# Denser filler work at the start, and another order of the mask, the gates and the router's product, in a fused mLSTM cell and mixture-of-depths kernel

## The chip, the cores and the metric

The kernel runs on one core of a Trainium2 chip. The metric is the device time of one execution in microseconds. Before the change it is 199.75 us, the median of three runs (199.61 to 199.81). The profile was taken of another execution, of 199.56 us; it spans 197.8 us from its first to its last instruction, and all positions in time below are counted from the start of that span.

A core has five engines that work side by side and wait for each other by semaphores. The profile calls them PE (TensorE, matrix products; PEld are its weight loads), DVE (VectorE), ACT (ScalarE), POOL (GpSimd) and SP (SyncE, which here issues transfers).

## The reference

Two blocks follow each other. The first is an mLSTM cell over 4 batches, 8 heads, 768 steps and a head dimension of 40:

```python
for t in range(S):
    m_new = np.maximum(f_gate[:, :, t] + m, i_gate[:, :, t])
    f_stab = np.exp(f_gate[:, :, t] + m - m_new)
    i_stab = np.exp(i_gate[:, :, t] - m_new)
    C = f_stab * C + i_stab * einsum('bhd,bhe->bhde', v_t, k_t)
    n = f_stab * n + i_stab * k_t
    y[:, :, t] = sigmoid(o_gate_t) * (C q_t) / max(|n . q_t|, 1)
```

The second is a mixture of depths on x, which is y with the heads side by side (4 x 768 x 320). Scores are x times a router's vector `w_gate`; in each batch the 128 rows of highest score go through a two-layer perceptron (320 to 1024 to 320, ReLU), and its output, times the sigmoid of the score, is added to them. All other rows are passed on.

## The kernel before

The kernel cuts each batch into 6 chunks of 128 steps, 24 chunks in all, and runs the recurrence in its chunked form. For a chunk it makes transposed q and k (`turn`, line 283, into T), their products pS (line 325), a matrix of decay weights W (`weights`, lines 303 and 304: a product pW of two small operands a_o and M_o, and an exponential on ScalarE), the causal mask of W (`causal`, line 309, GpSimd), the weighted products P (`weighted`, line 331, VectorE), the numerators pH (line 382), and the exchange with the state C (lines 351, 357, 364 to 374). The order of the program on each engine is the order in which the functions are called; each engine keeps it.

The prologue, which makes the first two chunks and the gates' running sums, is written out by hand, up to the first full `step`. Between its pieces stand fillers, products whose result nobody reads, which keep TensorE at work:

```python
def warm(n):
    pw = ps_c.tile([128, 4 * L], FP, name="pw", tag="c")
    for _ in range(n):
        nc.tensor.matmul(pw, earlier[:, 0:128], earlier[:, 0:4 * L], start=True, stop=True)
...
warm(6)
sums(0, nc.vector)                 # running sums of the gates, VectorE
maxima(0)
split(0, 1, nc.gpsimd)             # a in three bf16 parts
ends(0)                            # pe: three tiny products
warm(2)
split(0, 0, nc.vector, slice(0, BH))
carry(0)
T[0] = work.tile([128, 2, NP, L], FP, name="T")
turn(loaded[0][0], 0, T[0])        # four transposes of k, a copy by ScalarE
moving = operands(0, 0, [(ps_s, "s"), (ps_s, "s")], nc.vector)
moving()                           # M_o by VectorE
pm = carried(0)
turn(loaded[0][0], 1, T[0])        # the same of q
pg = ps_m.tile([128, DM], FP, name="pg", tag="m")
nc.tensor.matmul(pg, one, wg_row, start=True, stop=True)   # router's vector on all rows
...
W[0] = weights(0, 0)
causal(W[0])
level(0, pm)
split(0, 0, nc.vector)
pS[0] = products(T[0])
scales(0)                          # two exponentials, ScalarE
nc.scalar.copy(out=wg, in_=pg)
...
P[0] = weighted(pS[0], W[0])
...
moving = operands(0, 1, [(ps_m, "m"), (ps_m, "m")], nc.vector)
moving()
moving = operands(0, 2, [(ps_c, "c")], nc.vector)
...
turn(loaded[1][0], 0, T[1])
keep(0, columns(0))
```

`earlier` is a tile of ones, 128 x 768 in bf16, set by GpSimd; it is later the mask of the router's comparison, and the running sums read it too.

Operands of later chunks are made on ScalarE alone, as are the output gates:

```python
# operands(u, c, pools) without an engine: six small products into pO, then
nc.scalar.activation(out=a_o[u, c], in_=pO[1], func=AF.Identity, bias=of[:, 0:1], scale=1.0)
for h in range(4):
    nc.scalar.activation(out=M_o[u, c][:, h], in_=pO[0], func=AF.Identity, ...)

def gated(n):
    so = loaded[n][2]
    nc.scalar.activation(out=so, in_=so, func=AF.Tanh, scale=0.5)
    nc.scalar.add(so, so, 1.0)
```

In a step the outputs are scaled by the gates on GpSimd (`sor = so * rec`, line 397, in `norm`). The first full step is that of chunk 2, and is called with hooks:

```python
def step(n, first=False, **more):
    ...
    pH = within(P[n], v1)
    run(more.get("carry", ()))
    ...                                  # decay of C (POOL), products, exchange
    num, sor = norm(nums.get(n), pH, so)
    run(more.get("sor", ()))
    ...                                  # P and the state of the next chunk
    if n + 2 < N:
        stated(n + 2); W[n + 2] = weights(*steps[n + 2]); causal(W[n + 2])
    layer(b, c)                          # fillers, or the perceptron's products
    ... turned(n + 2) ... gated(n + 2) ... result, score, compare
    run(more.get("end", ()))
    if n == 2:
        operands(0, 5, [(ps_m, "m")])

def late():
    W[3] = weights(0, 3)
    operands(0, 4, [(ps_m, "m")])
    gated(2)
    gated(3)

step(2, first=True, carry=[late], sor=[lambda: causal(W[3])], end=[second_places])
```

So the mask of chunk 3 is called behind the scaling by the gates in this step.

Of the kernel before, what the change touches and what calls it, by code (L numbers as in the profile page):

```python
# [8 lines left out]
FP = mybir.dt.float32  # L9
BF = mybir.dt.bfloat16  # L10
# [11 lines left out]
def kernel(  # L22
# [20 lines left out]
    nc = tc.nc  # L43

    B, H, S, D = q.shape
    L = 128
# [4 lines left out]
    DM = H * D  # L51
# [15 lines left out]
    const = ctx.enter_context(tc.tile_pool(name="const", bufs=1))  # L67
# [8 lines left out]
    ps_h = ctx.enter_context(tc.tile_pool(name="ps_h", bufs=1, space=PSUM))  # L76
    ps_m = ctx.enter_context(tc.tile_pool(name="ps_m", bufs=2, space=PSUM))
# [6 lines left out]
    def load_gates(eng, dst, src, g):  # L84
        for c in range(3):
            t = slice((3 * g + c) * L, (3 * g + c + 1) * L)
            eng.dma_start(out=dst[g][c * BH:(c + 1) * BH], in_=src[:, :, t].rearrange("b h p -> (b h) p"))
# [3 lines left out]
    wg_row = const.tile([1, DM], FP, name="wg_row")  # L91
    nc.scalar.dma_start(out=wg_row, in_=moe_w_gate.rearrange("(o d) -> o d", o=1))
    load_gates(nc.scalar, f_sb, f_gate, 1)
    load_gates(nc.scalar, i_sb, i_gate, 1)
    earlier = const.tile([128, NT * L], BF, name="earlier")
    nc.gpsimd.memset(earlier, 1.0)
    ident = const.tile([128, 128], FP, name="ident")
# [35 lines left out]
    one = const.tile([1, 128], FP, name="one")  # L133
# [17 lines left out]
    for j in range(2):  # L151
        nc.vector.tensor_reduce(out=of[:, j:j + 1], op=OP.add, axis=AX.XY,
                                in_=ident.rearrange("p (g x) -> p g x", x=32)[:, :, 12 * j:12 * j + 12])
# [9 lines left out]
    m = gate.tile([BH, NT + 1], FP, name="m")  # L163
# [5 lines left out]
    def warm(n):  # L169

        pw = ps_c.tile([128, 4 * L], FP, name="pw", tag="c")
        for _ in range(n):
            nc.tensor.matmul(pw, earlier[:, 0:128], earlier[:, 0:4 * L], start=True, stop=True)  # L173

    def sums(g, eng):

# [45 lines left out]
    def operands(u, c, pools, eng=None):  # L222


        g, own = c // 3, slice(c % 3 * BH, c % 3 * BH + BH)
        pO = [pool.tile([128, 3 - len(pools), L], FP, name=f"pO{j}", tag=tag) for j, (pool, tag) in enumerate(pools)]
        pO = [pO[0][:, 0], pO[-1][:, len(pO) % 2]]
        for j in (1, 0):
            for part in range(3):
                nc.tensor.matmul(pO[j], place[j][u][own, part].rearrange("p g k h -> p (g k h)"),  # L230
                                 parts[j][g][part][own], start=(part == 0), stop=(part == 2))
        M_o[u, c] = const.tile([128, 4, L], BF, name=f"M_o{u}{c}")
        a_o[u, c] = const.tile([128, L], BF, name=f"a_o{u}{c}")
        nc.scalar.activation(out=a_o[u, c], in_=pO[1], func=AF.Identity, bias=of[:, 0:1], scale=1.0)
        if eng is None:
            for h in range(4):
                nc.scalar.activation(out=M_o[u, c][:, h], in_=pO[0], func=AF.Identity, scale=which[:, h:h + 1],  # L237
                                     bias=of_which[:, h:h + 1])
            return None

        def moving():
            eng.scalar_tensor_tensor(out=M_o[u, c], in0=pO[0].unsqueeze(1).to_broadcast([128, 4, L]),
                                     scalar=of[:, 1:2], in1=which.unsqueeze(2).to_broadcast([128, 4, L]),
                                     op0=OP.add, op1=OP.mult)
        return moving
# [15 lines left out]
    wg = const.tile([128, DM], FP, name="wg")  # L261
# [29 lines left out]
# [6 lines that stand above are left out]
    def weights(b, c):  # L297

        W = work.tile([128, H, L], FP, name="W")
        for h0 in range(0, H, 4):  # L300
            own = slice(64 * (b % 2) + 8 * h0, 64 * (b % 2) + 8 * h0 + 32)
            pW = ps_t.tile([128, 4, L], FP, name="pW", tag="t")
            nc.tensor.matmul(pW, a_o[b // 2, c][own], M_o[b // 2, c][own], start=True, stop=True)  # L303
            nc.scalar.activation(out=W[:, h0:h0 + 4, :], in_=pW, func=AF.Exp)  # L304
        return W

    def causal(W):
        for h0 in range(0, H, 4):
            nc.gpsimd.affine_select(out=W[:, h0:h0 + 4, :], in_=W[:, h0:h0 + 4, :], compare_op=OP.is_ge, fill=0.0, base=0,  # L309
                                    pattern=[[0, 4], [1, L]], channel_multiplier=-1)  # L310
# [66 lines left out]
    def within(P, v1):  # L377
        pH = ps_h.tile([128, H, DP], FP, name="pH", tag="h")
        for j in range(2):
            for p in range(NP):  # L380
                for t in HALVES:
                    nc.tensor.matmul(pH[t, 2 * p + j, :], P[:, p, j, t], v1[:, 2 * p + j, :], start=True, stop=True)  # L382
        return pH
# [144 lines left out]
    T, W, wv, state = {}, {}, {}, {}  # L528
# [3 lines left out]
    def load(n):  # L532
        if n < N:
            load_qk(n)
            load_v(n)
            load_so(n)
# [27 lines left out]
    def step(n, first=False, **more):  # L564
        b, c = steps[n]
        _, v1, so = loaded[n]
        load(n + AHEAD)
        pH = within(P[n], v1)
        run(more.get("carry", ()))

        soon = c == 0 or n == N - 1
        if n + 1 < N:
            decay(*steps[n + 1])
            if first:
                pS[n + 1] = products(T[n + 1])
            give = exchange(*steps[n + 1], loaded[n + 1][0], T[n + 1], wv[n + 1])
            if not first:
                pS[n + 1] = products(T[n + 1])
        if soon:
            pb, pc = steps[n - 1]  # L580
            spread(pc, *state[pb][1][:2])
        if c == 0:
            state[b] = open_batch()

        num, sor = norm(nums.get(n), pH, so)
        run(more.get("sor", ()))
        if n + 1 < N:
            if first:
                P[n + 1] = weighted(pS[n + 1], W[n + 1])
            nums[n + 1] = exchanged(*steps[n + 1], *give)  # L590
            if not first:
                P[n + 1] = weighted(pS[n + 1], W[n + 1])
        if soon:
            if c == 0:
                result(b, c, num, sor)
            compare(pc, *state[pb][1])
        if n + 2 < N:
            stated(n + 2)
            W[n + 2] = weights(*steps[n + 2])
            causal(W[n + 2])  # L600
        layer(b, c)
        if b > 0 and c == 1:
            picked[b - 1] = gather(b - 1, number(sel[b - 1], token))
        if n + 2 < N:
            turned(n + 2)
        if b > 0 and c == 0:
            pcol = columns_of(state[b - 1][1][2])
        elif b > 0 and c == 2:
            layers[b - 1] = Layers(b - 1, *picked[b - 1])
            layers[b - 1].enter()  # L610
        if not soon:
            pb, pc = steps[n - 1]
            spread(pc, *state[pb][1][:2])
        if n + 2 < N:
            gated(n + 2)
        if c > 0:
            result(b, c, num, sor)
        score(b, c, state[b][0])
        if not soon:
            compare(pc, *state[pb][1])  # L620
        run(more.get("end", ()))
        if b > 0 and c == 0:
            rank = ranks(pcol, state[b - 1][1][3])
            sel[b - 1] = mod.tile([128, NT, K_], HF, name="sel", bufs=1)
            select(sel[b - 1], rank, 0, NT)
        elif b > 0 and c == 2:
            layers[b - 1].gate()
            if b > 1:
                layers[b - 2].leave()
        if n == 2:  # L630
            operands(0, 5, [(ps_m, "m")])
        elif 3 <= n < 3 + NT:
            operands(1, n - 3, [(ps_m, "m")])
# [7 lines left out]
        load_v(n)  # L641
    load_so(AHEAD - 1)
    load(AHEAD)
    warm(6)

    sums(0, nc.vector)
    maxima(0)
    split(0, 1, nc.gpsimd)
    ends(0)
    warm(2)  # L650
    split(0, 0, nc.vector, slice(0, BH))
    carry(0)
    T[0] = work.tile([128, 2, NP, L], FP, name="T")
# [2 lines left out]
    moving()  # L656
    pm = carried(0)
    turn(loaded[0][0], 1, T[0])
    pg = ps_m.tile([128, DM], FP, name="pg", tag="m")
    nc.tensor.matmul(pg, one, wg_row, start=True, stop=True)  # L660
    for n in range(1, 4):
        pads(n, nc.gpsimd)
    W[0] = weights(0, 0)
# [2 lines left out]
    split(0, 0, nc.vector)  # L666
    pS[0] = products(T[0])
    scales(0)
    nc.scalar.copy(out=wg, in_=pg)

    sums(1, nc.gpsimd)
    P[0] = weighted(pS[0], W[0])
# [3 lines left out]
    moving = operands(0, 1, [(ps_m, "m"), (ps_m, "m")], nc.vector)  # L676
    moving()
    moving = operands(0, 2, [(ps_c, "c")], nc.vector)
    T[1] = work.tile([128, 2, NP, L], FP, name="T")
    turn(loaded[1][0], 0, T[1])  # L680
    keep(0, columns(0))
# [7 lines left out]
    num, sor = norm(None, pH, loaded[0][2])  # L689
# [31 lines left out]
    num, sor = norm(nums[1], pH, loaded[1][2])  # L721
# [11 lines left out]
    def late():  # L733

        W[3] = weights(0, 3)
        operands(0, 4, [(ps_m, "m")])
        gated(2)
        gated(3)

    def second_places():  # L740
        for j in range(2):
            nc.gpsimd.memset(place[j][1], 0.0)
        places(1)

    step(2, first=True, carry=[late], sor=[lambda: causal(W[3])], end=[second_places])
    for n in range(3, N):
        step(n)
        if n == 3:
# [99 lines left out]
```

## Time and profile before

| | |
|---|---|
| device time, median of 3 | 199.75 us |
| span of the profiled execution | 197.8 us |
| mean granted TensorE clock, as recorded | 0.988 |
| DVE / ACT / POOL busy | 146.3 / 102.0 / 102.3 us |
| fillers (line 173), all | 29, busy 10.2 us |
| transfers by the main queue | 22.34 MB |

The page gives the busy time of each engine, the span in 40 slices, the transfers, and the chain of work that ended last: beginning with the last instruction, each piece is followed back to what released it. A timeline row merges equal neighbours: its start, its length, the engine, the line of the kernel, the operation, output and inputs, the number of instructions, and in brackets the idle time of the engine before it and what ended that. A busy TensorE is not a fast one: the rate of its products is seen from how long a known piece of work takes. The stretches view gives for each window the busy time of the engines, the mean granted clock, the mean share of the 16 transfer engines, and GB/s.

### The profile page before, as it was taken

The numbers are of one execution on the slowest core, as the hardware profiler recorded it, in microseconds if no ns is written. First come the engines' busy times: TensorE is split into PE (matmuls) and PEld (weight loads), VectorE is DVE, ScalarE is ACT, GpSimd is POOL, SyncE is SP. The second block draws the span as 40 slices with busy tenths as digits, with TensorE's granted clock in tenths as the row PEclk, the third lists the DMA queues.
The fourth block names the chain that finished last, engine by engine and source line by source line (L and its number), as shares of the span: only waits on it lengthen the run. The fifth ranks groups of instructions, "written<-read, shape, count | busy, mean of one in ns | idle before, by whom it ended". The sixth has DMA issues, their size and how long they took to land.

```text
span 197.8 us, 6503 instructions
## 1 busy us (share of the span) xinstructions
PE 181.3 (92%) x2598; PEld 149.3 (75%) x2598; DVE 146.3 (74%) x412; ACT 102.0 (52%) x238; POOL 102.3 (52%) x167
## 2 busy tenths in 40 slices
PE   5999989099999999899999999999999899998990
PEld 1678867077778777798889778988798699968960
DVE  6654897339998999777999797879997788585101
ACT  0554658547888957765663544566436544301110
POOL 6563784764548578325555854256557552023202
PEclk9999999969999999999999999999999999999998
DMA  4999999464999999999999499299994111010100
GB/s 78 152 148 135 164 155 160 58 114 55 219 241 174 157 214 230 173 178 169 155 157 156 64 174 175 63 174 123 162 145 90 37 36 36 35 36 35 33 0 33
DMA packets 105713, 24.21 MB, mean 122 GB/s; under 512 B 100626, under 2 KB 105107, under 8 KB 105683
## 3 DMA queue, kind: packets, MB, share of 16 engines
q1 hardware_dynamic: 104864, 22.34, 73.7%
q0 software_dynamic: 384, 1.31, 2.0%
q8 instruction: 20, 0.33, 0.8%
q10 hardware_dynamic: 434, 0.15, 0.7%
q14 instruction: 11, 0.08, 0.2%
HBM read 19.20 MB, written 4.59 MB: 120 GB/s over the span
## 4 chain that ended last, share of the span: by engine, by line
PE 73%; issue 8%; DVE 5%; DMA 4%; ACT 4%; POOL 4%; POOLq 1%; SPq 0%; DVEq 0%
PE pS L325 13%; PE pH L382 12%; PE pt L283 11%; PE ph L496 9%; PE pIC L351 5%; PE py L505 5%; PE pIC L357 4%; PE pW L303 4%; PE pw L173 3%; PE pO L230 3%; ACT T L284 2%; DMA out_dram<-ye,idx 2%; PE pb L414 1%; DMA xe<-out_dram,idx 1%; POOL W L309 1%
## 5 line engine op out<-in xcount | busy, mean ns | idle before, releaser
L397 POOL TENSOR_TENSOR sor<-so,rec 128x320 f32<-128x320 f32 x24 | 17.8, 741 | 50.4 <-DVE rec L395 38.5
L309 POOL TENSOR_SCALAR_AFFINE_SELECT W<-W 128x512 f32<-128x512 f32 x48 | 34.7, 747 | 13.9 <-ACT W L304 13.9
L304 ACT ACTIVATE W<-pW 128x512 f32<-128x512 f32 x48 | 26.0, 594 | 29.9 <-PE pW L303 21.2
L284 ACT COPY T<-pt 128x512 f32<-128x512 f32 x48 | 26.1, 589 | 22.2 <-PE pt L283 22.2
L331 DVE TENSOR_TENSOR P<-pS,W 128x512 f32<-128x512 f32 x48 | 30.9, 686 | 7.4 <-POOL W L309 4.2
L325 PE MATMUL pS<-T 64*128 64x128 f32 x384 | 28.8, 291 | 0.0
L283 PE MATMUL pt<-ident,qk 128*128 128x128 f32 x192 | 28.7, 295 | 0.0
L382 PE MATMUL pH<-v,P 128*64 128x64 f32 x768 | 28.5, 229 | 0.0
L421 DVE SCALAR_TENSOR_TENSOR ge<-sb,sc,earlier 128x128 bf16<-128x128 f32 (+5 forms) x23 | 16.9, 735 | 15.5 <-ACT sb L415 15.0
L382 PEld LDWEIGHTS pH<-v,P 128*64 128x64 f32 x768 | 25.1, 141 | 3.3 <-issue 1.0
L283 PEld LDWEIGHTS pt<-ident,qk 128*128 128x128 f32 x192 | 23.4, 151 | 5.2 <-ACT W L304 2.3
L325 PEld LDWEIGHTS pS<-T 64*128 64x128 f32 x384 | 24.1, 193 | 2.5 <-issue 1.2
L496 PE MATMUL ph<-xeT,w 128*128 128x128 f32 x192 | 23.8, 280 | 0.0
L496 PEld LDWEIGHTS ph<-xeT,w 128*128 128x128 f32 x192 | 22.1, 192 | 1.7 <-issue 1.6
L505 PE MATMUL py<-w,hT 128*128 128x320 f32 x64 | 19.3, 442 | 0.0
L408 DVE CUSTOM_DVE_ANT_0 scr<-x,wg 128x320 f32<-128x320 f32 x24 | 16.8, 698 | 0.7
L173 PE MATMUL pw<-earlier 128*128 128x512 bf16 x29 | 10.2, 475 | 6.4 <-DVE C L374 4.7
L316 POOL TENSOR_TENSOR wv<-v,cols 128x328 f32<-128x328 f32 x20 | 14.8, 740 | 2.2 <-DVE cols L257 2.2
L505 PEld LDWEIGHTS py<-w,hT 128*128 128x128 f32 x64 | 11.5, 191 | 5.0 <-issue 1.4
L351 PE MATMUL pIC<-C,T 128*64 128x82 f32 x320 | 15.0, 235 | 0.0
L511 POOL DMA_INDIRECT out_dram<-ye,idx x4 | 4.6, 1142 | 20.1 <-DVE ye L509 20.1
L237 ACT ACTIVATE M_o<-pO,of_which,which 128x128 bf16<-128x128 f32 x36 | 13.5, 461 | 0.0
(138 smaller groups left out, 274.5 us busy)
## 6 DMA issues: line engine op xcount, KB each, us to landing
qk<-in_k_dram SPq DMA_DIRECT2D x24, 160.0 KB, 4.1
qk<-in_q_dram SPq DMA_DIRECT2D x24, 160.0 KB, 4.7
v<-in_v_dram SPq DMA_DIRECT2D x24, 160.0 KB, 5.0
so<-in_o_gate_dram SPq DMA_DIRECT2D x24, 160.0 KB, 4.5
out_dram<-x SPq DMA_DIRECT2D x24, 160.0 KB, 2.5
w<-in_moe_w_dram SPq DMA_DIRECT2D x2, 640.0 KB, 6.2
w<-in_moe_w_dram SPq DMA_DIRECT2D x2, 512.0 KB, 4.6
w<-in_moe_w_dram SPq DMA_DIRECT2D x1, 256.0 KB
```

Source lines behind the costliest of these rows:

```text
L283: nc.tensor.transpose(pt[:, p, :], qk[:, j, 2 * p:2 * p + 2, :].rearrange("s a d -> s (a d)"), ident)
L284: nc.scalar.copy(out=T[:, j], in_=pt)
L304: nc.scalar.activation(out=W[:, h0:h0 + 4, :], in_=pW, func=AF.Exp)
L309: nc.gpsimd.affine_select(out=W[:, h0:h0 + 4, :], in_=W[:, h0:h0 + 4, :], compare_op=OP.is_ge, fill=0.0, base=0, pattern=[[0, 4], [1, L]], ...
L325: nc.tensor.matmul(pS[j][:, p, :], T[e, 0, p, :], T[e, 1, p, :], start=True, stop=True)
L331: nc.vector.tensor_tensor(out=P[:, :, j, :], in0=pS[j], op=OP.mult, in1=W.rearrange("p (n a) t -> p n a t", a=2)[:, :, j, :])
L351: nc.tensor.matmul(pI[t, 2 * p * D1:2 * (p + 1) * D1], T[:, 1, p, t], C[:, p].rearrange("e a d -> e (a d)"), start=True, stop=True)
L382: nc.tensor.matmul(pH[t, 2 * p + j, :], P[:, p, j, t], v1[:, 2 * p + j, :], start=True, stop=True)
L397: nc.gpsimd.tensor_tensor(out=sor, in0=so, in1=rec.unsqueeze(2).to_broadcast([128, H, D]), op=OP.mult)
L421: nc.vector.scalar_tensor_tensor(out=ge[:, GE[u]:GE[u + 1]], in0=sb.rearrange("p t l -> p (t l)")[:, 0:n], scalar=sc[:, u:u + 1], in1=earl ...
L496: nc.tensor.matmul(self.ph[:, f % 4, :], w1[:, j, f * 128:(f + 1) * 128], self.xeT[:, j, :], start=(j == 0), stop=(j == NDC - 1))
L505: nc.tensor.matmul(self.py, self.hT[:, f, :], w2[:, f, :], start=(f == 0), stop=(f == NFC - 1))
```

## The change

The change has three parts. First, the fillers read a tile of their own, `fill`, which VectorE sets as its first work, in place of `earlier`, and there are more of them in the prologue: 9 for 6, 3 for 2, and one where the router's product stood. Second, that product and the copy of its result to SBUF come later, after the operands of chunk 2, and use another PSUM bank. Third, in the first full step, the causal mask of chunk 3 is called ahead of the scaling by the gates, and ahead of the decay of C; the gates of chunk 2 are made ahead of the operands of chunk 4; and the gates of chunk 3 move to the end of the step. The number of fillers in the later steps stays. The computation is the same.

What it is for: to keep TensorE densely at work from the first microsecond, to take a slow product out of the chain at the start, and to undo an order in which engines wait for each other in the first full step.

```diff
@@ prologue: tiles
     load_gates(nc.scalar, i_sb, i_gate, 1)
+    fill = const.tile([128, 4 * L], BF, name="fill")
+    nc.vector.memset(fill, 1.0)
     earlier = const.tile([128, NT * L], BF, name="earlier")
@@ def warm(n)
-            nc.tensor.matmul(pw, earlier[:, 0:128], earlier[:, 0:4 * L], start=True, stop=True)
+            nc.tensor.matmul(pw, fill[:, 0:128], fill, start=True, stop=True)
@@ prologue
-    warm(6)
+    warm(9)
 
     sums(0, nc.vector)
     maxima(0)
     split(0, 1, nc.gpsimd)
     ends(0)
-    warm(2)
+    warm(3)
@@
     turn(loaded[0][0], 1, T[0])
-    pg = ps_m.tile([128, DM], FP, name="pg", tag="m")
-    nc.tensor.matmul(pg, one, wg_row, start=True, stop=True)
+    warm(1)
@@
     scales(0)
-    nc.scalar.copy(out=wg, in_=pg)
@@
     moving = operands(0, 2, [(ps_c, "c")], nc.vector)
+    pg = ps_h.tile([128, DM], FP, name="pg", tag="h")
+    nc.tensor.matmul(pg, one, wg_row, start=True, stop=True)
+    nc.scalar.copy(out=wg, in_=pg)
     T[1] = work.tile([128, 2, NP, L], FP, name="T")
@@ def late()
         W[3] = weights(0, 3)
+        causal(W[3])
+        gated(2)
         operands(0, 4, [(ps_m, "m")])
-        gated(2)
-        gated(3)
@@
-    step(2, first=True, carry=[late], sor=[lambda: causal(W[3])], end=[second_places])
+    step(2, first=True, carry=[late], end=[lambda: gated(3), second_places])
```

## The prediction

> **What bounds the kernel now.** I read the page's busy shares first, then the chain of waits that ended last, then the timeline of two stretches, 0 to 25 us and 30 to 48 us, and last the granted clock in short windows.
>
> ```profile
> PE 181.3 (92%) x2598; PEld 149.3 (75%) x2598; DVE 146.3 (74%) x412; ACT 102.0 (52%) x238; POOL 102.3 (52%) x167
> ...
> PE 73%; issue 8%; DVE 5%; DMA 4%; ACT 4%; POOL 4%; POOLq 1%; SPq 0%; DVEq 0%
> ```
>
> The first line is the busy time of each engine, the second the chain by engine. TensorE (PE) is both: 92% busy and 73% of the chain. From 46 us to 171 us the chain is nearly pure TensorE work, step after step. So a microsecond won before 46 us should simply move all the rest earlier; the change touches only what lies before.
>
> Now the start. Columns: start, length, engine, line, operation, tiles, count, and in brackets the idle time before and what ended it.
>
> ```profile
> 1.60 2.74 PE L173 MATMUL pw<-earlier 128*128 128x512 bf16 x6 [1.60 <-POOL earlier L96]
> ...
> 10.90 2.08 PE L325 MATMUL pS<-T 64*128 64x128 f32 x16
> ...
> 16.23 1.98 PE L382 MATMUL pH<-v,P 128*64 128x64 f32 x32
> ...
> 19.35 1.16 PE L325 MATMUL pS<-T 64*128 64x128 f32 x16
> ...
> 24.57 1.15 PE L382 MATMUL pH<-v,P 128*64 128x64 f32 x32
> ```
>
> The same work, pS, takes 2.08 us at 10.9 and 1.16 us at 19.35; pH takes 1.98 us at 16.2 and 1.15 us at 24.6. TensorE runs at about half rate until some 18 to 19 us. The clock column of the page reads full there, so the durations have to be trusted and not the column, which seems to have no record yet.
>
> The second stretch:
>
> ```profile
> 33.24 1.52 ACT L237 ACTIVATE M_o<-pO,of_which,which 128x128 bf16<-128x128 f32 x4
> ...
> 35.14 0.47 ACT L295 ACTIVATE so<-so 128x320 f32<-128x320 f32 x1
> ...
> 35.69 0.72 POOL L397 TENSOR_TENSOR sor<-so,rec 128x320 f32<-128x320 f32 x1 [2.02 <-ACT so L295]
> ...
> 37.62 1.29 DVE L331 TENSOR_TENSOR P<-pS,W 128x512 f32<-128x512 f32 x2 [3.69 <-POOL W L309]
> ...
> 39.94 1.46 PE L173 MATMUL pw<-earlier 128*128 128x512 bf16 x3 [4.75 <-DVE C L374]
> ```
>
> A convoy: ScalarE (ACT) makes M_o of chunk 4 before it makes the gates `so` of chunk 2; GpSimd (POOL) waits 2.02 us for them, and behind it, at 36.37, stands the mask of chunk 3, whose input was ready at 33.1. VectorE waits 3.69 us for that mask, TensorE 4.75 us for VectorE's C. After so long a gap the clock drops:
>
> ```profile
> 39.00:40.00 1.00, 0.06 (x1) 0.06 (x2) 0.95 (x4) 0.00 (x0) 1.00 (x3) 0.68 0.00 0
> 40.00:41.00 1.00, 1.00 (x3) 0.45 (x4) 0.91 (x3) 0.00 (x0) 1.00 (x3) 0.50 0.00 0
> ...
> 42.00:43.00 1.00, 1.00 (x7) 0.87 (x5) 0.00 (x0) 0.58 (x1) 0.58 (x1) 0.61 1.00 160
> ```
>
> The third number from the end is the granted clock. A mean of 0.68 is 0.36 us at full and 0.64 at half rate, 0.61 is 0.78 us at half rate: it was halved from about 39.36 to 42.78, 3.42 us.
>
> [...] TensorE is at work almost without a break from 5 to 16 us, much of it transposes, and stays slow. [...]
>
> Counting windows of 3.41 us back from 39.36 gives edges at 1.82, 5.23, 8.64. In the first, the six fillers fill 2.5 us (74%) and did not raise the clock; from 39.36 to 42.78 TensorE was busy from 39.94 on (83%) and it rose. [...]
>
> **The change, part by part.**
>
> *Fillers.* They read a tile of their own, set by VectorE's first instruction. VectorE's 192-element memsets take 0.22 us and its 384-element one 0.38, so 256 words take about 0.27 us: from 0.92 to 1.20, and fillers start at about 1.25 in place of 1.60. VectorE has 0.54 us of idle time before the gates land at 3.5, so its chain does not move. A slow filler takes 0.43 us (9 would be 3.84 us): they run to 5.1, 96% of the window 1.82 to 5.23. With three more after pe, any window starting from 0.65 to 4.1 is at least 82% full, so the phase of the grid should hardly matter. The clock should rise at 5 to 7 us in place of about 18.9.
>
> *What full rate is worth.* Before, the chain holds 11.9 us of TensorE from 6.33 to 18.21. It cannot all halve, since other engines then set the pace. Walking through: first transposes end at 6.8 in place of 7.18, but T waits for ScalarE's table load until 7.5 as before. The M_o product starts at 7.25 (was 7.97), the second T copy at 8.35 (was 9.22), as q's transposes no longer end at 9.18. One filler stands where pg, the router's product, was (1.25 us of chain); the exponentials start at 8.95 (was 11.01), pS ends at 10.3 (was 12.98), P starts at 10.8 when GpSimd's masks are done (was 13.08). Two operand groups, pg at its new place (about 0.65 us), transposes and columns end at 13.0 (was 16.3). pH takes 1.1 and ends at 14.1 (was 18.21), the next exponentials start at 14.4 (was 18.78), the mask ends at 16.25 (was 20.67), P of chunk 1 starts at 16.3 (was 20.70). Gain **4.3 us**. From there to 33 us the chain runs over GpSimd, ScalarE and VectorE at their own speed and just moves.
>
> *Chunk 3.* I keep the old time axis. ScalarE: W to 33.1, gates of chunk 2 to 34.1, then a_o and M_o of chunk 4 to 35.85. GpSimd: wv to 32.98, mask to 34.2 (was 37.6), decay of C to 34.95, sor to 35.7. VectorE: P 34.25 to 35.55, num, C done at 36.55 (was 39.88). TensorE's pW needs M_o: 35.9 in place of 34.8, still ahead of C. Fillers start at 36.55 (was 39.94), the gap is two short ones and the clock stays up, so three fillers and eight transposes take 1.85 us and not 3.06. The transposes end at 38.4 in place of 43.0: 4.6 us.
>
> *Given back.* In the next step ScalarE has copies, exponentials and two gates (chunks 4 and 3) before M_o of chunk 5: 37.8 + 1.2 for copies + 0.3 for sb + 1.95 for the gates + 1.85 gives 43.1, while TensorE has done pS at 42.05 and waits 1.1 us; a further 0.2 us in the next. ScalarE's load in a step is about 5.2 us against 5.5 of TensorE, so it catches up. Part 2: 4.6 - 1.3 = **3.3 us**.
>
> The sum: 199.75 - 4.3 - 3.3 = 192.15; I put 192.4, since a walk through a timeline finds fewer waits than there are.
>
> **Rivals.** *A. The clock does not rise early.* Then pe starts 0.2 later, one more filler between costs 0.43, one in place of pg saves 0.8, pg costs 1.25 where it lands: about +1, and only part 2 gains: 197.5. [...] Against: the fillers are the densest work there is. *B. The loads become the bound.* Each 160 KB issue takes about 1 us and lands 4 to 5 us later; q of chunk 2, issued at 9.8, lands near 14.7 and is wanted at 16.2, so 1.5 us are left, and for later chunks more. It would cost at most 1 us: 193.4. *C. ScalarE stays the bound after step 2* and keeps another 1 to 2 us: 194. Its 52% mean says no, its 95% in steps 3 to 8 says maybe. *D. The gain in chunk 3 is larger* since the late gates cost nothing: 191.
>
> **Range and chances.** C and B put the upper side at 194, A at 197.5 with about one in ten; D with a little more in the prologue gives 190.3. Two per cent is 195.76: only A with a bad part 2 gets there.
>
> **What would show it.** Right: pS of chunk 0 in about 1.15 us; fillers from 1.25 us; P of chunk 0 at about 11 and of chunk 1 at 16.3; the mask of chunk 3 ahead of sor; no half-rate record near 32 to 36 us; TensorE idle there under 2 us at a time; a wait of pW for M_o of about 1 us in the step after. Wrong: pS still near 2 us (A), transposes waiting for a load (B), or pW waiting for M_o in several steps (C).

## The result, and the profile after

The changed kernel takes 192.94 us, the median of four runs (191.18 to 194.48); before it was 199.78 (199.61 to 200.02, four runs beside them). The ratio is 0.9627, with a 95% interval of 0.9545 to 0.971. The interval leaves out the slowest run of the change, 194.48 us; medians and ranges are of all runs.

The page of the changed kernel, engines and chain (which this time can be followed back only to 37.9 us):

```profile
PE 176.4 (93%) x2603; PEld 144.9 (76%) x2603; DVE 148.3 (78%) x413; ACT 102.2 (54%) x238; POOL 102.9 (54%) x167
...
PE 62%; issue 7%; ACT 3%; DMA 3%; DVE 2%; POOLq 1%; POOL 1%
```

TensorE still sets the pace: its busy time fell from 181.3 to 176.4 us though five more products are recorded, since products of the start that ran at half rate before, as pS in 2.08 us, now run at full rate. Its timeline at the start (columns as in the prediction; line numbers are two or three higher than before):

```profile
0.99 0.48 DVE L96 MEMSET fill<- 128x512 bf16 x1 [0.99 <-PEq L838]
...
1.53 4.02 PE L175 MATMUL pw<-fill 128*128 128x512 bf16 x9 [1.53 <-DVE fill L96]
...
9.99 1.16 PE L327 MATMUL pS<-T 64*128 64x128 f32 x16
```

The first pS now takes 1.16 us, full rate, and not 2.08. The fillers, however, start at 1.53 us and not at 1.25. The first entry of the trace's clock record, the rise to full rate (called the rise below), is at 7.31 us; before, it was at 18.88 us.

The first full step:

```profile
29.76 1.23 POOL L311 TENSOR_SCALAR_AFFINE_SELECT W<-W 128x512 f32<-128x512 f32 x2
...
31.02 1.29 DVE L333 TENSOR_TENSOR P<-pS,W 128x512 f32<-128x512 f32 x2 [0.37 <-POOL W L311]
...
32.49 0.39 PE L305 MATMUL pW<-M_o,a_o 32*128 32x512 bf16 x2 [1.09 <-ACT M_o L239]
...
33.34 0.82 PE L175 MATMUL pw<-fill 128*128 128x512 bf16 x3 [0.45 <-DVE C L376]
```

The mask follows its exponential (28.84 to 29.92), VectorE waits 0.37 us for it and not 3.69, TensorE 0.45 us for C and not 4.75. What came instead is a wait of 1.09 us for M_o.

Where the 7.4 us of span went, from three marks in the two timelines. The first mark, before and after, is this row (before, then after):

```profile
32.02 1.09 ACT L304 ACTIVATE W<-pW 128x512 f32<-128x512 f32 x2 [0.82 <-PE pW L303]
28.84 1.08 ACT L306 ACTIVATE W<-pW 128x512 f32<-128x512 f32 x2 [0.82 <-PE pW L305]
```

| mark | before | after | gained so far |
|---|---|---|---|
| exponential of chunk 3 starts | 32.02 | 28.84 | 3.18 |
| eight transposes behind the fillers of step 2 end | 43.01 | 35.03 | 7.98 |
| fillers of step 3 start | 46.99 | 39.64 | 7.35 |
| span | 197.8 | 190.4 | 7.4 |

All of it is won before 40 us; behind that everything only moves.

### The profile page after: what moved, and what is told of

It reads as the page before. It is cut to its first block, busy times and chain, and to the rows that moved or that the text cites. A ratio compares the mean times of both kernels' runs of the same rounds, so it can differ in the third digit from the quotient of the medians.

```text
span 190.4 us, 6514 instructions
## 1 busy us (share of the span) xinstructions
PE 176.4 (93%) x2603; PEld 144.9 (76%) x2603; DVE 148.3 (78%) x413; ACT 102.2 (54%) x238; POOL 102.9 (54%) x167
## 3 DMA queue, kind: packets, MB, share of 16 engines
q0 software_dynamic: 384, 1.31, 2.2%
## 4 chain that ended last, share of the span: by engine, by line
PE 62%; issue 7%; ACT 3%; DMA 3%; DVE 2%; POOLq 1%; POOL 1%
PE pS L327 11%; PE pH L384 11%; PE ph L498 9%; PE pt L285 8%; PE py L507 5%; PE pIC L353 5%; PE pIC L359 4%; PE pW L305 3%; PE pw L175 2%; ACT T L286 2%; DMA out_dram<-ye,idx 2%; DMA xe<-out_dram,idx 2%; PE pb L416 1%; PE pO L232 1%; DVE ge L423 1%
## 5 line engine op out<-in xcount | busy, mean ns | idle before, releaser
L311 POOL TENSOR_SCALAR_AFFINE_SELECT W<-W 128x512 f32<-128x512 f32 x48 | 35.3, 760 | 11.0 <-ACT W L306 10.9
L327 PE MATMUL pS<-T 64*128 64x128 f32 x384 | 27.9, 285 | 0.0
L384 PE MATMUL pH<-v,P 128*64 128x64 f32 x768 | 27.6, 225 | 0.0
L384 PEld LDWEIGHTS pH<-v,P 128*64 128x64 f32 x768 | 24.3, 138 | 3.1 <-issue 1.0
L285 PE MATMUL pt<-ident,qk 128*128 128x128 f32 x192 | 26.2, 277 | 0.0
L285 PEld LDWEIGHTS pt<-ident,qk 128*128 128x128 f32 x192 | 21.4, 141 | 5.2 <-ACT W L306 2.3
L327 PEld LDWEIGHTS pS<-T 64*128 64x128 f32 x384 | 23.3, 187 | 2.3 <-issue 1.0
L175 PE MATMUL pw<-fill 128*128 128x512 bf16 x34 | 11.6, 470 | 2.0 <-DVE fill L96 1.5
```

Source lines behind the costliest of these rows:

```text
L285: nc.tensor.transpose(pt[:, p, :], qk[:, j, 2 * p:2 * p + 2, :].rearrange("s a d -> s (a d)"), ident)
L327: nc.tensor.matmul(pS[j][:, p, :], T[e, 0, p, :], T[e, 1, p, :], start=True, stop=True)
```

## Experiments

Rise and mark are of the profiled run: the first rise in its clock record, and the start of chunk 3's exponential (in "fillers only" and "best, no middle" a fall of the clock, told of below, lies ahead of the mark and delays it). Where more than one change of the clock is quoted from a profile here, the changes lie near whole multiples of 3.41 us apart: in before 20.48 (18.88 to 39.36) and 3.41, in fillers only 20.48 (6.08 to 26.56), 6.82, 3.42 and 3.41. A window, below, is 3.41 us counted from such a change, and the grid is the row of them. Three groups of four kernels ran, in the order of the table, each group beside before on one chip; a kernel of one group is compared with one of another with less certainty. Before had medians of 199.76, 199.81 and 199.87 us there, but its single runs went from 195.27 to 202.57. Its row is of the first group.

| kernel | median us | range | runs | rise us | mark us |
|---|---|---|---|---|---|
| before | 199.76 | 195.27-202.57 | 42 | 18.88 | 32.02 |
| prologue only | 196.79 | 195.56-197.43 | 6 | 7.05 | 28.70 |
| chunk 3 only | 194.57 | 192.28-195.29 | 6 | 17.16 | 31.40 |
| router's product only | 200.14 | 195.35-203.16 | 22 | 19.60 | 32.51 |
| fillers only | 197.28 | 195.59-198.39 | 21 | 6.08 | 29.55 |
| mask only | 191.75 | 190.57-193.12 | 6 | 4.28 | 27.62 |
| middle fillers | 192.10 | 191.40-193.48 | 6 | 5.20 | 27.84 |
| zero fill | 191.69 | 190.88-193.59 | 6 | 7.08 | 28.58 |
| old counts | 195.53 | 192.11-198.63 | 22 | 19.67 | 32.52 |
| best | 190.94 | 190.50-192.67 | 6 | 5.57 | 27.83 |
| best, no middle | 191.29 | 190.59-192.11 | 6 | 5.74 | 28.96 |
| more fillers | 193.86 | 192.75-195.96 | 6 | 7.05 | 29.82 |
| changed, again | 192.76 | 191.27-193.98 | 6 | 5.63 | 28.06 |

### The two parts apart

The change's prologue with the old order of chunk 3 (in these cuts several lines of code may stand on one):

```diff
-        W[3] = weights(0, 3); causal(W[3]); gated(2); operands(0, 4, ...)
+        W[3] = weights(0, 3); operands(0, 4, ...); gated(2); gated(3)
-    step(2, first=True, carry=[late], end=[lambda: gated(3), second_places])
+    step(2, first=True, carry=[late], sor=[lambda: causal(W[3])], end=[second_places])
```

> The change's prologue with the old order of chunk 3. Theory (the two parts add: the early clock is worth 3.2 us, read at the exponential of chunk 3, and the order of chunk 3 some 4.2 us with the half-rate window behind it): 196.5 us, the 4.7 us gap of TensorE before the fillers of step 2 stays, and the clock is halved after it. Rival (the early clock also removes the later gap, or the gap swallows what the prologue won): 192.5 or 199.5 us.

196.79 us, 3.0 under before's median, as the theory said. Six of before's 42 runs, though, took 195.27 to 197.36 us, and the new prologue alone is no faster than these: its own took 195.56 to 197.43. The mean recorded clocks of the two sets agree as well: 0.980 in the four shortest of before and the two shortest here, 0.974 in before's other two, and 0.974 and 0.971 in the two longest here. This fits a prologue that makes the early rise the rule, where before has it in a few runs; those short runs of before were not profiled.

In the timeline the wait of TensorE for C is there as before. A row of the stretches view over the end of this wait shows what it brings (the second number behind the window is PE's busy time, the third from the end the clock):

```profile
36.62 0.61 PE L175 MATMUL pw<-fill 128*128 128x512 bf16 x1 [4.74 <-DVE C L376]
...
44.41 0.82 PE L175 MATMUL pw<-fill 128*128 128x512 bf16 x2
```

```profile
34.36:37.77 3.41, 0.94 (x2) 0.51 (x4) 3.18 (x8) 0.00 (x0) 3.41 (x8) 0.50 0.47 73
```

The clock is halved for two windows here, 34.36 to 41.19 us, where before lost one: TensorE was at work for 0.70 us of the window ahead (30.94 to 34.36) and for 0.94 us of this one.

The old prologue with the new order:

```diff
-        W[3] = weights(0, 3); operands(0, 4, ...); gated(2); gated(3)
+        W[3] = weights(0, 3); causal(W[3]); gated(2); operands(0, 4, ...)
-    step(2, first=True, carry=[late], sor=[lambda: causal(W[3])], end=[second_places])
+    step(2, first=True, carry=[late], end=[lambda: gated(3), second_places])
```

> The old prologue with the new order of chunk 3. Theory: 199.8 - 4.2 = 195.6 us, the mask of chunk 3 right behind its exponential, TensorE idle about 1.1 us and then 0.45 us instead of 4.75, no half-rate window there. Rival (without the early clock, the order gains only the wait and not the window): 197 us.

```profile
11.00 2.08 PE L325 MATMUL pS<-T 64*128 64x128 f32 x16
...
35.89 0.82 PE L173 MATMUL pw<-earlier 128*128 128x512 bf16 x2 [0.45 <-DVE C L374]
...
42.18 0.82 PE L173 MATMUL pw<-earlier 128*128 128x512 bf16 x2
```

194.57 us. The start is slow, the long wait is gone, and from the mark to the fillers of step 3 it takes 42.18 - 31.40 = 10.78 us, as the changed kernel (39.64 - 28.84 = 10.80) and against 14.97 before. The order of chunk 3 is worth 4.2 us with the old prologue, and the rival, which would have lost 1.4 of it, is out. With the new prologue it is worth 4.9 in the profiles (44.41 - 28.70 = 15.71 in prologue only against 10.80), as two windows at half rate follow the wait there and not one.

By medians, 3.0 and 5.2 make 8.2, and the whole brings about 7. By the profiles, at the fillers of step 3, the parts make 2.58 + 4.81 = 7.39 against 7.35, where 0.62 of the 4.81 is the earlier mark of chunk 3 only (31.40), whose clock rose at 17.16. With six runs each, spread over 1.9 and 3.0 us, it stays open whether the parts add. The spread itself led to the question of the half-rate windows below.

### What in the prologue counts

```diff
-    pg = ps_m.tile(...); nc.tensor.matmul(pg, one, wg_row, ...)      # behind q's transposes
-    nc.scalar.copy(out=wg, in_=pg)
     moving = operands(0, 2, [(ps_c, "c")], nc.vector)
+    pg = ps_h.tile(...); nc.tensor.matmul(pg, one, wg_row, ...); nc.scalar.copy(out=wg, in_=pg)
```

> Only the router's product and its copy moved behind the operands of chunk 2. Theory (the gain of the prologue comes from the clock): the 1.25 us saved ahead of the exponentials are paid back behind the operands, still at half rate; 199.3 us, pS of chunk 0 still near 2.0 us. Rival (the prologue's gain is that of the router's product leaving the chain): 197 us.

200.14 us, near the theory. pS starts 0.51 us sooner, at half rate as before, and the mark comes 0.49 us later, at 32.51. Moving the product brings no gain while the clock is down:

```profile
10.39 2.08 PE L325 MATMUL pS<-T 64*128 64x128 f32 x16
```

```diff
+    fill = const.tile([128, 4 * L], BF, name="fill"); nc.vector.memset(fill, 1.0)
-            nc.tensor.matmul(pw, earlier[:, 0:128], earlier[:, 0:4 * L], ...)
+            nc.tensor.matmul(pw, fill[:, 0:128], fill, ...)
-    warm(6) ... warm(2)
+    warm(9) ... warm(3)
```

> Only the fillers: own tile, 9 and 3 in place of 6 and 2; the router's product stays where it was. Theory (clock): pS of chunk 0 in about 1.16 us, clock up at 5 to 9 us, 197.0 us, some 0.5 us less of a gain than the whole prologue since the router's product stands in the chain at about 0.65 us. Rival (router's product): 200.5 us, since the extra fillers only delay the first transposes by 0.8 us.

197.28 us with the first pS in 1.16 us at 9.38: the fillers alone bring 2.5 of the prologue's 3.0 us. Its profile has something that nobody expected:

```profile
27.00 1.98 PE L384 MATMUL pH<-v,P 128*64 128x64 f32 x32
```

pH at half rate again, though the clock had risen at 6.08. The record says half rate from 26.56 to 33.38 (and again, behind the wait for C, from 36.80 to 40.21). In the window ahead, 23.15 to 26.56, TensorE was busy for 2.30 of 3.41 us, mostly with transposes and the small products of the operands.

The numbers of fillers alone, with the own tile and the moved product kept:

```diff
-    warm(9) ... warm(3) ... warm(1)
+    warm(6) ... warm(2) ...
```

> The changed kernel with the old numbers of fillers in the prologue (6, 2 and none where the router's product stood), still from their own tile. Theory (it is the number, that is the density of the first windows, that makes the clock rise early in nearly all runs; with six it does only when the grid of windows falls well): a two-peaked spread, median 195 us, some runs below 191.5. Rival (the own tile, or moving the router's product, is enough): 192.9 us, as the changed kernel.

195.53 us, and a spread over 6.5 us: 3 of 22 runs at 192.1 to 192.3, most at 194.7 to 195.8. Chunk 3 only, with neither the own tile nor the moved product, took 194.57. So these two don't do it; the number of fillers does. That with six fillers the clock rises early only now and then fits the spread, and so do before's six short runs; none of these was profiled.

```diff
-    warm(9) ... warm(3)
+    warm(12) ... warm(5)
```

> The changed kernel with 12 and 5 fillers in place of 9 and 3. Theory (9 and 3 already make the clock rise in the first windows; any more only delay pe and the first transposes, by three fillers of 0.43 us ahead of pe, and two of 0.22 behind it): 1.0 to 1.7 us slower, 194.3 us. Rival (denser is better still, the rise comes surer): 192 us.

193.86 us, 1.1 above the changed kernel of the same group, as the theory said. The mark is at 29.82 with the rise at 7.05, where the change's prologue has 28.70 with the same rise: 1.12 us for three fillers more ahead of pe and two behind it. Nine are enough.

```diff
-    nc.vector.memset(fill, 1.0)
+    nc.vector.memset(fill, 0.0)
```

> The changed kernel with the fillers' tile set to 0.0 in place of 1.0, which becomes a 256-word memset and should take about 0.27 us in place of 0.48. Theory (the clock follows activity, not values, and the memset's length is 0.2 us of start): fillers from about 1.3 us, clock up at 5 to 9 us, pS of chunk 0 in 1.16 us, 0 to 0.2 us faster: 192.8 us. Rival (products of zeros do not count as work): pS of chunk 0 near 2.0 us and 194.6 us or more.

```profile
0.94 0.27 DVE L96 MEMSET fill<- 128x256 uint32 x1 [0.94 <-PEq L838]
```

Zeros are set as words, in 0.27 us against 0.48; the fillers start at 1.26 and the first pS takes 1.16 us. The clock rose with products of zeros as well. With the rise at 7.08 the mark is at 28.58: 0.26 us ahead of the changed kernel's, whose clock rose 0.23 us later, and 0.12 ahead of prologue only's, whose clock rose at 7.05. So the shorter memset is worth some 0.1 us. The median, 191.69, is 1.1 us under that of the changed kernel in the third group, but the ranges overlap and six runs on another chip don't fix that.

### What in chunk 3 counts

```diff
         W[3] = weights(0, 3)
         causal(W[3])
-        gated(2)
         operands(0, 4, [(ps_m, "m")])
+        gated(2)
+        gated(3)
-    step(2, first=True, carry=[late], end=[lambda: gated(3), second_places])
+    step(2, first=True, carry=[late], end=[second_places])
```

> The changed kernel, but in the first full step only the mask of chunk 3 stands ahead; the operands of chunk 4 come ahead of the gates as before, and both gates stay there. Theory (what counts is that the mask no longer stands behind a scaling that waits for the gates; the order on ScalarE does not matter or even costs): within 0.7 us of the changed kernel, 192.3 to 193.3 us, and the waits of pW for M_o (1.09 and 0.55 us in the changed kernel) go. Rival (gates ahead of operands carry the gain, since the outputs and so the buffers are late otherwise): 196 us.

```profile
28.54 1.22 POOL L311 TENSOR_SCALAR_AFFINE_SELECT W<-W 128x512 f32<-128x512 f32 x2
...
31.30 0.72 POOL L399 TENSOR_TENSOR sor<-so,rec 128x320 f32<-128x320 f32 x1 [0.83 <-ACT so L297]
```

The scaling waits 0.83 us for the gates again, and it costs nothing, since no mask stands behind it. The waits for M_o shrink from 1.09 and 0.55 us to 0.23 and none; those for C grow from 0.45 to 1.31 us, and a new one of 0.48 us comes in step 3. From the mark to the fillers of step 3: 38.35 - 27.62 = 10.73 us against 10.80. With the mask ahead, all of the gain is there; the order on ScalarE, which the change moves as well, adds nothing to it. Whether that order alone, with the mask still behind the scaling, would have won it too was not run. The median is 191.75.

### The windows in the middle

```diff
-    def warm(n):
+    def warm(n, pool=ps_c, tag="c"):
     turned(3)
+    warm(2, ps_s, "s")
```

> The changed kernel with two fillers more, behind the transposes of chunk 3, where TensorE has 0.7 us of idle time before the columns; their PSUM tile is one that is free there. Theory (runs with only the new prologue lose one or two windows of 3.41 us at half rate that begin near 26.6 or 34.4 us, behind stretches thin in products; the same makes the spread of the changed kernel, 191.2 to 194.5 us): the slower runs go, median 191.5 us, no run above 193. Rival (the spread comes from elsewhere, as the moment of the first rise): median 193 us, spread as before.

192.10 us, 191.40 to 193.48. The highest run is the profiled one, and its profile has a window at half rate from 32.51 to 35.92, behind the waits for M_o and C of step 2. But its span is only 190.6 us: 2.9 us of its time lie outside the program's instructions, against about 1.7 in most runs. By spans the six runs lie within 189.7 to 190.8 us, while four of the twelve runs of mask only and zero fill, on the same chip, have 191.4 to 191.9. So the slower runs are gone, as the theory said, as far as six runs can show it. One thin stretch was filled and another remained; the last versions treat both.

```diff
-    nc.vector.memset(fill, 1.0)
+    nc.vector.memset(fill, 0.0)
     ... only the mask ahead, as above ...
     turned(3)
+    warm(2, ps_s, "s")
     ... fillers of the first full step:
-                warm(3)
+                warm(3, ps_s, "s")      # pS of chunk 3, read long before C is done
```

> All that the runs point to, on the changed kernel: fillers' tile of zeros, only the mask moved ahead in the first full step, two fillers behind the transposes of chunk 3, and the fillers of the first full step in a PSUM tile that VectorE has long read, so that they run in the gap instead of behind it. Theory: 0.3 us from the start, 0.1 from ScalarE's order, about 0.2 from the gap, and fewer half-rate windows: median 191.0 us, highest below 193. Rival (the half-rate windows in the middle come from something else): 191.7 us with some runs at 193.5.

```profile
30.95 0.82 PE L175 MATMUL pw<-fill 128*128 128x512 bf16 x2
```

The fillers of step 2 no longer wait for C. 190.94 us, 0.9582 of before (0.9531 to 0.9633); the changed kernel beside it took 192.76 us, 0.9667 (0.9618 to 0.9717). By spans the two don't overlap: 188.8 to 189.5 us against 189.6 to 192.3. The gap itself gave nothing: fillers of step 3 start 10.73 us behind the mark, as with the mask only. TensorE now waits 1.06 us ahead of the transposes behind these fillers.

The same without the two fillers behind `turned(3)`:

> The same without the two fillers behind the transposes of chunk 3. Theory (those two fill the thin stretch near 23 to 27 us): some runs are 1.3 to 2.5 us slower than the best, with a half-rate stretch beginning at 25 to 28 us; median 191.3 us. Rival (the fillers in the gap are enough): no difference, 191.0 us.

191.29 us. The medians are too close to tell, but the profile shows the very thing, in a run of 192.11 us: pH, and the stretches 25 to 31 us.

```profile
26.42 1.98 PE L384 MATMUL pH<-v,P 128*64 128x64 f32 x32
```

```profile
25.00:28.00 3.00, 2.28 (x36) 1.86 (x35) 2.72 (x9) 2.03 (x6) 0.97 (x2) 0.70 1.23 212
28.00:31.00 3.00, 3.00 (x30) 2.41 (x28) 1.04 (x4) 2.04 (x6) 2.11 (x4) 0.50 1.44 143
```

Half rate from 26.22 to 33.05. None of the best kernel's six runs has a mean clock under 0.993; two of these six have 0.981. Their spans are 190.3 and 190.4 us, the other four 188.9 to 189.6.

The changed kernel once more, without an edit:

> The changed kernel once more, for more runs of it beside the others on one chip: 191.2 to 194.5 us, median 192.9 us, as before.

192.76 us, 191.27 to 193.98, as expected. With the clock up at 5.63 us the mark is at 28.06. Over the ten runs of the changed kernel, here and in the result, the time follows the mean recorded clock: 191.2 to 191.3 us at 1.000, 191.8 to 192.1 at 0.994, 192.5 to 193.0 at 0.988, 193.6 to 194.5 at 0.977 and 0.978. Over 192 us, 0.978 means 2 x 0.022 x 192 = 8.4 us at half rate, and the first profiled run, with 0.994, had 2.2 us, all in the tail: the difference is near two windows of 3.41 us. Where they lie in those runs was not seen; in the profiles above such windows lie between 26 and 41 us. The moment of the first rise is not in this mean, and can differ between these runs too.

## Why the prediction was right, point by point

**What bounds the kernel.** Right. What was won by 40 us, 7.35, is the span's 7.4.

**Fillers.** The memset was sized from VectorE memsets of zeros, which go as words (192 of them in 0.22 us); a tile of bf16 ones took 0.48 us instead of 0.27, and the fillers started at 1.53 instead of 1.25. The clock was to rise at 5 to 7 us; with nine fillers and three the profiled runs have 4.28 to 7.31. That a window some four fifths full would do agrees with mask only: the window of 3.41 us that ended at its rise of 4.28 had fillers from 1.53 on, 2.75 us or 81%, where no rise followed before's 74%. It was an estimate; that the share decides is not shown, and the last section has windows that speak against it. The place of the grid differs from run to run: the two profiles of the changed kernel have the rise at 7.31 and 5.63. All rises with nine fillers and three lie within 3.03 us, less than one window, and those of the kernels with few fillers, 17.16 to 19.67, within 2.51.

**What full rate is worth.** Predicted 4.3 (the walk's own last step, 20.70 to 16.3, is 4.4), measured 3.18 in this profile. The walk had the rise near 5.2. By the table, prologues of the change gain 3.2 us at a rise of 7.31, 4.0 at 5.63, 4.2 at 5.20 and 4.4 at 4.28 (mark against 32.02). The mechanism held, and its size for a rise where the walk had it; what was mis-sized is the place of the grid, which differs from run to run, and some 0.1 us of memset with it. P of chunk 0 started at 11.73 and not 10.8, P of chunk 1 at 17.43 and not 16.3.

**Chunk 3.** Predicted 4.6 up to the transposes: 7.98 - 3.18 = 4.80. **Given back**: predicted 1.3, measured 7.98 - 7.35 = 0.63. TensorE waited 0.55 us and not 1.1 for M_o in step 3, and not at all in the next. Net 4.2 instead of 3.3. So that the sum came out so near is luck: two errors of opposite sign, 1.1 too much in the prologue and 0.9 too little here. The mechanism of each part held. The prediction's reading of the late gates as part of the cause was half wrong: the mask-only kernel shows that they may stay late once the mask doesn't stand behind them.

**Rivals.** A, no early rise, did not come for the change in its profiled runs; it is what the profiles of before and of the kernel with old counts show. B: no transposes of the prologue waited for a load. C: waits for M_o of 1.09 us in step 2 and 0.55 in step 3, then none. D was nearer than its place in the text: chunk 3 brought more than the sum.

**What was not foreseen.** "No half-rate record near 32 to 36 us" held in the profile shown, but not in that of more fillers, whose edits leave this stretch as it is (half rate from 34.35 to 37.77). Behind stretches thin in dense products, at 23 to 35 us, the clock fell in four profiles: at 26.22 (best, no middle), 26.56 (fillers only), 32.51 (middle fillers) and 34.35 (more fillers). In the two of the changed kernel it did not. That it depends on where the grid falls is an estimate from the windows in the last section. That the changed kernel spreads over 3 us agrees with this, by the mean clocks of its runs and by the spans of the kernels with fillers in these stretches; that each of the slower runs has its windows there is argued, not shown.

## What to carry to other kernels

Try dense filler work at the very start: here, with nine fillers and three, the profiled runs had the clock up at 4.28 to 7.31 us, with six and two at 17.16 to 19.67, while twelve and five cost 1.1 us more than nine and three. Then look for later stretches thin in dense products: behind such stretches the clock fell again here, at 26.22 to 34.35 us in four profiles. When a wait is long, ask what stands behind the waiting instruction in its engine's order: moving the one item that others need, here a mask, ahead of it was worth 4.2 us, and hastening what it waited for added nothing to that. Where a kernel's runs spread over some microseconds, compare the clock record and the span of several runs before trusting small differences.

## What the hardware showed beyond what was expected

- Busy time alone does not decide whether the clock falls. Four profiles have a window over the same piece of step 2, with TensorE busy for 1.85 to 1.89 of 3.41 us (54 to 55%). The clock fell behind it where the fillers at its end had run for 0.06 us (more fillers, 30.94 to 34.36) and 0.18 us (middle fillers, 29.10 to 32.51). It did not fall where they had run for 0.39 us (changed again, 29.52 to 32.94) and 0.82 us (the changed kernel, below). It also fell behind 2.30 us (67%) of transposes and small products (fillers only, 23.15 to 26.56). Whether transposes count otherwise than the other small products was not shown; no run here separates them.

```profile
31.20:34.60 3.40, 1.85 (x19) 1.22 (x16) 3.32 (x8) 2.33 (x6) 2.84 (x5) 1.00 0.93 145
```

- Nor does it decide whether the clock rises: before had TensorE busy throughout from 5.23 to 15.47 us, three windows, much of it transposes, and rose only at 18.88.
- The clock rose at 7.08 us with products of zeros (zero fill), and at 7.31 and 5.63 with products of ones (the changed kernel).
- The clock column reads 1.00 ahead of the record's first entry, also where pS runs at half rate for 2.08 us.
- One kernel, before, took 195.3 to 202.6 us in 42 runs on one chip; the kernel with old counts 192.1 to 198.6 in 22. Three of before's runs, at 202.5 to 202.6 us, stay unexplained.
